# Batch 3's keys and queries loaded ahead of the down weights, and block sums at other places in VectorE's order

## The chip, the cores and the metric

The kernel runs on one core of one Trainium2 chip. The metric is the device time of one execution in microseconds, as the median of several runs. The profile is of one execution; its span is the time from the first to the last instruction, a little shorter than the device time.

Engine names as in the profile: PE is TensorE, PEld its weight loads, DVE VectorE, ACT ScalarE, POOL GpSimd, SP SyncE. DMAs that POOL issues are on queue q0, those of SP on q1; both are served by the same 16 DMA engines.

## What is computed

Sigmoid attention over 8 batches, 12 heads, 448 tokens, head size 64, and behind it a gated feed-forward layer (768 to 1536 to 768) over the 3584 tokens.

```
scores = scale * (q @ k^T) - log(S)
attn   = 1 / (1 + exp(-scores))
x      = (attn @ v), heads side by side            # [3584, 768]
gate   = max(x @ w_gate, 0);  val = x @ w_val
out    = (gate * val) @ w_out                       # float32
```

## The kernel before

All instructions of an engine run in the order in which the kernel's Python code emits them (a manual schedule), and the engines meet through semaphores. The order between attention and feed-forward work is written out by hand, batch by batch.

**Attention.** A batch's 12 heads go as three groups of four, its 448 tokens as seven chunks of 64, so a batch has 21 score units (group, chunk). `qk_unit` makes one unit: score matmuls into two PSUM banks (L239), a sigmoid on ACT (L187) into a tile PT. After a group's seven units `pv` (L257) multiplies with v and DVE copies the result, scaled, to `xT` (L184). PSUM has eight banks that are handed out in a ring, so each product waits until the bank that was given out eight allocations earlier has been read.

**Inputs.** `load` and `load_v` are DMAs on POOL's queue that convert to fp16. There is one buffer for keys and queries from batch 2 on (batch 1 has its own) and there are two for v; so a batch's keys can be loaded when the previous batch's have been rearranged. `dma_transposes(b, g)` rearranges keys and queries of group g on DVE (two copies into a tile `rel`, L222) and issues one DMA transpose on SP's queue (L226) into `qkT`. There are two `rel` buffers and three `qkT` buffers. `hold(b, g)` is a small copy on POOL that reads `qkT`, so that POOL's later DMA issues wait until that transpose has landed.

**Feed-forward.** For batch 0 and the first eight of 12 feature blocks of batch 0 and 1 the products are made in the plain or in a split form; later batches go in pairs. The split and paired forms are block products of Strassen's kind: seven products in place of eight, for which DVE makes sums of blocks ahead: `early_sum_steps` (weights, in batch 1), `split_sums` (batch 1's x, L391 X), `weight_sums(i)` (the down weights `wo`, L391 T), `token_sums` (four sums over hT, L441 and L391), `gate_sums` and `unit_sums`. `gv` is a plain unit: gate product, value product, ACT's relu (L334), DVE's product into `hT` (L343), which sets the value's bank free. `gv_split` is four units at once (L708 for PE, L719, L723 and L729 for DVE). `down_pair` is the output layer for two tiles of 128 tokens (PE L400; DVE L447 and L470; ACT L452), then stores on SP's queue.

**Order by batch.** A loop over `b` from 1 has stages `m`, each a burst of score units (`burst`) and then feed-forward work: in batch 1 `ffn_mix`, which pops plain units from a queue and emits, after each, one step of the early sums (from the second stage on); later `next_work`, which takes an item off `work` and emits `jobs` beside it. In batch 2 the items are the plain unit 8 (m = 0), the split units 0 to 3 (m = 1), plain unit 9 (m = 2), split 4 to 7 (m = 3), plain 10 and 11 (m = 4 and 5), all of batch 1's feed-forward. Batch 3 begins with `down_pair` of the first tiles. `prepare`, at the end of an item, emits the sums for the next one.

Before the change, DVE's order ran so: `split_sums(1)` after the plain unit of m = 0; the copies of `dma_transposes(3, 0)` and `(3, 1)` ahead of the unit of m = 4; `weight_sums(0)` and `(1)` after that unit; the token sums of the first tiles after the unit of m = 5; the copies of `(3, 2)` at the start of batch 3. POOL's order ran: v of batch 2, the down weights `wo`, then keys, queries and v of batch 3, then `hold(3, 2)` and batch 4's loads.

Of the kernel before, what the change touches and what calls it, by code (L numbers as in the profile page):

```python
# [18 lines left out]
def kernel(  # L19
# [10 lines left out]
    nc = tc.nc  # L30
# [82 lines left out]
    def load_v(b):  # L113
        v16 = tiles_of(b)[2]
        nc.gpsimd.dma_start(v16[:, 0::2, :], rows_of(v, b)[:, 0::2, :])
        for r in range(2):
            nc.gpsimd.dma_start(
                v16[64 - 64 * r : P - 64 * r, 1::2, :], rows_of(v, b)[64 * r : 64 * r + 64, 1::2, :]
            )
# [42 lines left out]
    def load_o():  # L162
        for m0, m1 in ((0, 512), (512, DM)):
            nc.gpsimd.dma_start(
                wo[:, :, m0:m1], moe_w_out[:, m0:m1].rearrange("(c p) m -> p c m", p=P)
            )
# [223 lines left out]
    def sub(o, a, b):  # L390
        nc.vector.tensor_tensor(out=o, in0=a, in1=b, op=AOP.subtract)  # L391
# [18 lines left out]
    def weight_sums(i):  # L410
        T = [late["T"][:, j] for j in range(4)]
        B11, B21 = wo[:, 0:HF, 0:HM], wo[:, HF:NFC, 0:HM]
        B12, B22 = wo[:, 0:HF, HM:DM], wo[:, HF:NFC, HM:DM]
        sub(T[i], *((B12, B11), (B22, T[0]), (B22, B12), (B21, T[1]))[i])
# [19 lines left out]
        return blocks  # L434

    def token_sums(g, p, k0=0, k1=HF):
        if ("y", g, p) not in sums:
            sums[("y", g, p)] = sums_tile(P)
        S1, S2, S4 = (t[:, k0:k1, :] for t in sums[("y", g, p)])
        A11, A12, A21, A22 = (t[:, k0:k1, :] for t in token_blocks(g, p))  # L440
        nc.vector.tensor_tensor(out=S1, in0=A21, in1=A22, op=AOP.add)  # L441
        sub(S2, S1, A11)
        sub(S4, A12, S2)
        sub(A21, A11, A21)

    def scaled(o, ps):
        nc.vector.tensor_scalar(  # L447
# [109 lines left out]
    def early_sum_steps(j, f):  # L557
        views = []
        for i in range(3 * j, 3 * j + 3):
            t = early.tile([P, 2, 512], FP16, tag=f"PT{i}", name="S")  # L560
            flat = t[:].rearrange("p a y -> p (a y)")[:, 0 : HD * 2 * P]
            views.append(flat.rearrange("p (x y) -> p x y", y=2 * P))
        yield lambda: gate_sums(f, f + 2)
        yield from unit_sum_steps(("s", f), f, views)
# [196 lines left out]
        c0, c1 = HALVES[half]  # L761
        push_gv(0, 64 * c0, 64 * (c1 - c0), fs, act_relu)

    def ffn_mix(count, hooks=(), steps=()):
        hooks = list(hooks)
        for left in range(count, -1, -1):
            while hooks and hooks[0][0] >= left:
                hooks.pop(0)[1]()
            if left:
                gv_queue.popleft()()  # L770
                for step in itertools.islice(steps, 1):
                    step()


# [80 lines left out]
    def hold(b, g):  # L855
        nc.gpsimd.tensor_copy(gate[0:1, :], qkT_tiles[(b, g)][0:1, 0, 0:2])
# [5 lines left out]
    def late_loads():  # L862
        dma_transposes(2, 2)
        hold(2, 2)
        load_v(2)
        load_o()


# [16 lines left out]
    def prepare():  # L885
        if work:
            kind, g, i = work[0]
            if kind == "w":
                unit_sums(("w", g, i), i)
            elif kind == "y":  # L890
                token_sums(g, i, 0, HF - 2 if FRESH.get(g) == i else HF)

    def next_work(jobs=(), alone=False, amid=None):
        kind, g, i = work.popleft()

        due = pending[:]
        del pending[:]

        def beside():
            for job in due + list(jobs):  # L900
                job()

        if kind == "y":
            down_pair(g, i, beside, prepare, not work, scaled_act if alone else scaled, amid)
        elif amid:
            raise ValueError(kind)
        elif kind == "w":
            gv_pair(g, i, lambda: (prepare(), beside()), nc.scalar.copy if alone else nc.vector.tensor_copy)
        elif kind == "s":
            gv_split(g, i, lambda: (prepare(), beside()))  # L910
        elif kind == "u":
            gv(g, 0, S, i, True)
            beside()
            prepare()
        else:
            beside()
            prepare()
            for m0, m1 in (DOWN_CUTS[i : i + 1] if g == 0 else ((0, 512), (512, DM))):
                down(g, 2 * NPP, m0, m1)

    for b in range(1, B):
        if b == 1:
            cuts, pv_at = (0, 3, 6, 9, 13, 17, 21), {3: (0, 2), 5: (1, 2)}
        else:
            cuts, pv_at = (0, 4, 7, 11, 14, 18, 21), {0: (-1, 2), 2: (0, 2), 4: (1, 2)}
        bursts = list(range(len(cuts) - 1))
        inner = {}
        if b > 2:
            inner = {0: 1, 3: 5} if b == 3 else {0: 1} if b % 2 == 0 else {2: 3, 3: 5} if b == B - 1 else {4: 5}
            for n in inner.values():  # L930
                bursts.remove(n)
        count = len(bursts)
        hooks = {}
        if b == 1:
            mix = (4, 3, 3, 3, 3, 4)
            hooks = {
                1: [(3, lambda: both(1, 1))],
                3: [(3, lambda: both(1, 2))],
                4: [(3, lambda: dma_transposes(2, 0)), (1, lambda: dma_transposes(2, 1))],
                5: [(4, late_loads)],  # L940
            }
            steps = itertools.chain.from_iterable(early_sum_steps(j, 2 * j) for j in range(4))
        else:
            mix = (0,) * count

        def burst(n):
            for i, (g, c) in enumerate(order[cuts[n] : cuts[n + 1]]):
                if n in pv_at and i == pv_at[n][1]:
                    if n == 0:
                        pv_finish(b - 1)  # L950
                        if b == 2:
                            push_group(0)
                        elif b % 2 == 0:
                            push_group(b // 2 - 1)
                    else:
                        pv_group(b, pv_at[n][0])
                qk_unit(b, g, c)

        if b == 3:
            dma_transposes(3, 2)  # L960
        for m in range(count):
            jobs = []
            burst(bursts[m])
            if m == 0 and b > 3:
                jobs.append(lambda: dma_transposes(b, 2))
            if b == 2 and m == count - 2:
                dma_transposes(3, 0)
                dma_transposes(3, 1)
            elif b == 3 and m == count - 1:
                jobs.append(lambda: dma_transposes(4, 1))  # L970
            elif 0 <= m - count + 2 and 3 < b < B - 1:
                jobs.append(lambda: dma_transposes(b + 1, m - count + 2))
            if b == 1:
                if m == 0:
                    load(2, 0, 1, "kq")
                    load(2, 1, 2, "kq")
                    load(2, 2, 3, "kq")
            elif m == 0 and b + 1 < B:
                if b == 3:
                    jobs.append(lambda: hold(3, 2))  # L980
                for g0, g1 in ((0, 1), (1, NG)) if b == 3 else ((0, NG),):
                    jobs.append(lambda g0=g0, g1=g1: load(b + 1, g0, g1, "kq"))
                jobs.append(lambda: load_v(b + 1))
            if b == 2 and m == 0:
                jobs.append(lambda: split_sums(1))
            elif b == 2 and m == 4:
                open_late()
                jobs.append(lambda: (weight_sums(0), weight_sums(1)))
            elif b == 3 and m == 0:
                jobs.append(lambda: (weight_sums(2), weight_sums(3)))  # L990
            elif b == 3 and m < 3:
                jobs.append(lambda: gate_sums(6 + 2 * m, 8 + 2 * m))
            if b % 2 and b > 2:
                if m == count - 1:
                    jobs.append(lambda: (batch_sums_t1(b // 2), batch_sums(b // 2, (0, 1))))
            elif b > 3 and m == 0:
                jobs.append(lambda: batch_sums(b // 2 - 1, (1, HD)))
            if mix[m]:
                for job in jobs:
                    job()  # L1000
                ffn_mix(mix[m], hooks.get(m, ()), steps if m else ())
            else:
                next_work(
                    jobs,
                    amid=(lambda: burst(inner[m])) if m in inner else None,
                )
            if b == 3 and m == count - 2:
                dma_transposes(4, 0)
# [35 lines left out]
```

## Time and profile before

| | |
|---|---|
| device time, median of 3 runs | 392.11 us (392.07 to 392.82) |
| profiled run: device time | 392.25 us |
| profiled run: span | 390.5 us |
| PE busy | 382.1 us |
| DVE busy | 299.6 us |
| ACT busy | 228.2 us |
| POOL busy | 50.0 us |
| granted TensorE clock, mean | 0.999 |

A row of the timeline reads: start and length in us, engine, line, operation, output<-inputs, shape, count, and in brackets the engine's idle time ahead of it with what ended it. Rows that follow one another closely are merged with a count. A length on PE holds pipelined matmuls, so the distance between two starts says more than the length. A row of DMA issues ends with the KB of one and the time from issue to landing; one that belongs to a line or tile gives the issue's own length in ns (least, median, most), then its start. A queue's row gives packets, MB and the share of 16 engines' time.

Batch 1's loop runs from about 30 to 61 us of the span, batch 2's from 61.7 to 97, batch 3's from 97 to 125.

### The profile page before, as it was taken

How to read it: one execution, taken by the hardware profiler on the slowest of the kernel's cores; microseconds unless marked ns; L12 is line 12 of the kernel's file. 1: busy time of each engine (PE TensorE's matmuls, PEld its weight loads, DVE VectorE, ACT ScalarE, POOL GpSimd, SP SyncE). 2: the span in 40 equal slices, each digit the busy share in tenths (PEclk: the TensorE clock that was granted, in tenths of full speed). 3: DMA queues.
4: the chain of work that ended last, by engine and by line, in shares of the span. 5: the costliest groups of instructions: out<-in, count | busy, mean ns of one | idle time of the engine just before them, and what ended most of it. 6: DMA issues, size and time to landing. Idle time of an engine off the chain costs nothing.

```text
span 390.5 us, 8971 instructions
## 1 busy us (share of the span) xinstructions
PE 382.1 (98%) x3576; PEld 223.8 (57%) x3576; DVE 299.6 (77%) x593; ACT 228.2 (58%) x482; POOL 50.0 (13%) x74
## 2 busy tenths in 40 slices
PE   7999999999999999999999999999999999999995
PEld 5678776884555545454555554545455555555663
DVE  3454666859867789999757789999987788999563
ACT  5967787567787755555547774545467354333321
POOL 9633305200220300003000300000000000000000
PEclk9999999999999999999999999999999999999999
DMA  9999997998499892225945694132002230000335
GB/s 179 198 200 204 204 184 128 205 203 141 71 210 229 159 219 34 48 49 70 187 91 129 122 227 76 29 65 43 10 21 74 72 81 1 2 0 2 81 86 159
DMA packets 68987, 43.81 MB, mean 112 GB/s; under 512 B 35664, under 2 KB 65616, under 8 KB 68944
## 3 DMA queue, kind: packets, MB, share of 16 engines
q0 software_dynamic: 30496, 23.24, 39.3%
q1 hardware_dynamic: 37664, 19.24, 23.3%
q10 hardware_dynamic: 784, 0.75, 0.6%
q8 instruction: 28, 0.46, 0.4%
q14 instruction: 15, 0.12, 0.1%
HBM read 47.19 MB, written 11.01 MB: 149 GB/s over the span
## 4 chain that ended last, share of the span: by engine, by line
PE 90%; ACT 4%; DVE 3%; DMA 1%; issue 1%; DVEq 0%; ACTq 0%
PE u L400 33%; PE g L400 16%; PE y L400 10%; PE qk_ps L239 8%; PE pv_ps L257 8%; PE g_ps L322 4%; PE v_ps L322 4%; ACT PT L187 3%; PE u L708 2%; PE g L708 1%; PE ya L366 1%; PE trt L204 1%; DMA ysb<-in_k_dram 1%; PE yb L366 1%; DVE S L391 1%
## 5 line engine op out<-in xcount | busy, mean ns | idle before, releaser
L187 ACT ACTIVATE PT<-qk_ps 128x448 f16<-128x448 f32 (+3 forms) x318 | 151.3, 585 | 81.3 <-PE qk_ps L239 80.8
L400 PEld LDWEIGHTS <-S 128*128 128x128 f16 x558 | 54.6, 98 | 45.3 <-issue 0.7
L627 DVE TENSOR_TENSOR gsb<-g,gsb 128x448 f32<-128x448 f32 x72 | 42.8, 624 | 10.1 <-PE g L400 9.6
L239 PE MATMUL qk_ps<-qkT 64*64 64x448 f16 (+2 forms) x756 | 47.8, 336 | 1.8 <-DMA qkT<-rel 0.7
L400 PEld LDWEIGHTS <-hT 128*128 128x128 f16 x306 | 28.5, 98 | 22.7 <-issue 5.2
L623 ACT COPY gsb<-u 128x448 f32<-128x448 f32 x48 | 25.6, 558 | 24.0 <-PE u L400 22.9
L257 PE MATMUL pv_ps<-PT,v 64*64 64x448 f16 (+2 forms) x756 | 37.3, 329 | 0.2 <-DVE hT L343 0.2
L184 DVE TENSOR_SCALAR xT<-pv_ps 128x448 f16<-128x448 f32 (+2 forms) x53 | 27.8, 566 | 9.6 <-PE pv_ps L257 8.4
L452 ACT ACTIVATE ysb<-u 128x384 f32<-128x384 f32 x30 | 14.7, 490 | 34.5 <-PE u L400 29.6
L400 PEld LDWEIGHTS <-wg 128*128 128x128 f16 x216 | 20.1, 98 | 21.8 <-issue 4.3
L400 PEld LDWEIGHTS <-wv 128*128 128x128 f16 x216 | 21.1, 98 | 19.7
L239 PEld LDWEIGHTS <-qkT 64*64 64x64 f16 x756 | 17.9, 105 | 22.4 <-issue 14.2
L470 DVE SCALAR_TENSOR_TENSOR ysb<-y,ysb 128x384 f32<-128x384 f32 x29 | 16.1, 556 | 17.9 <-PE y L400 10.4
L257 PEld LDWEIGHTS <-v 64*64 64x64 f16 x756 | 21.9, 107 | 11.2 <-issue 1.4
L400 PE MATMUL u<-T,hT 128*128 128x384 f16 x132 | 25.1, 327 | 0.0
L111 POOL DMA_DIRECT2D k<-in_k_dram x14 | 10.8, 774 | 108.1 <-DVE rel L222 103.0
L343 DVE TENSOR_TENSOR hT<-gate_sb,v_ps 128x256 f16<-128x256 f32 (+2 forms) x28 | 11.6, 419 | 16.6 <-ACT gate_sb L334 8.9
L400 PE MATMUL u<-xT,wg 128*128 128x448 f16 x108 | 23.5, 354 | 0.0
L400 PE MATMUL g<-xT,S 128*128 128x448 f16 x108 | 23.4, 352 | 0.0
L400 PE MATMUL u<-X,S 128*128 128x448 f16 x108 | 23.4, 352 | 0.0
L400 PE MATMUL g<-X,S 128*128 128x448 f16 x108 | 23.4, 352 | 0.0
L400 PE MATMUL u<-xT,wv 128*128 128x448 f16 x108 | 23.4, 352 | 0.0
(94 smaller groups left out, 574.6 us busy)
## 6 DMA issues: line engine op xcount, KB each, us to landing
out_dram<-ysb SPq DMA_DIRECT2D x52, 192.0 KB, 3.0
v<-in_v_dram POOLq DMA_DIRECT2D x8, 336.0 KB, 14.7
v<-in_v_dram POOLq DMA_DIRECT2D x16, 168.0 KB, 14.3
k<-in_k_dram POOLq DMA_DIRECT2D x4, 672.0 KB, 11.1
q<-in_q_dram POOLq DMA_DIRECT2D x4, 672.0 KB, 15.2
k<-in_k_dram POOLq DMA_DIRECT2D x9, 224.0 KB, 12.1
q<-in_q_dram POOLq DMA_DIRECT2D x7, 224.0 KB, 12.4
wo<-in_moe_w_out_dram POOLq DMA_DIRECT2D x1, 1536.0 KB, 12.1
```

What stands on the lines that cost most here:

```text
L184: nc.vector.tensor_scalar(out=xT, in0=src, scalar1=XSCALE, scalar2=None, op0=AOP.mult)
L187: nc.scalar.activation(PT_ap, ps_ap, AF.Sigmoid, bias=sig_bias, scale=qk_scale)
L239: nc.tensor.matmul(out_of(hh)[o : o + 64, :], qkT[rows, c, cols], qkT[rows, NCH + c0 : NCH + c1, cols], start=True, stop=True, tile_positi ...
L257: nc.tensor.matmul(ps[hh][64 * r : 64 * r + 64, 0:qn], v16[rows, 2 * g + hh, c * D : (c + 1) * D], pieces[c][rows, hh, :], start=(c == 0), ...
L322: nc.tensor.matmul(ps[:, 0:qn], (wg, wv)[i][:, dc, f * P : (f + 1) * P], xT_tiles[b][:, dc, q0 : q0 + qn], start=(dc == 0), stop=(dc == ND ...
L343: nc.vector.tensor_tensor(out=hT_tiles[g][:, f, o : o + qn], in0=gate_sb[:, 0:qn], in1=ps[1][:, 0:qn], op=AOP.mult,)
L400: nc.tensor.matmul(ps[:, 0:n], A[:, k_, :], W[:, k_, :], start=(first and k_ == 0), stop=(k_ == kn - 1), skip_group_check=True,)
L452: nc.scalar.activation(o, ps[:, 0:HM], AF.Copy, scale=OUT_SCALE)
L470: nc.vector.scalar_tensor_tensor(out=o, in0=ps[:, 0:HM], scalar=OUT_SCALE, in1=o, op0=AOP.mult, op1=AOP.add)
L623: by(gs[u][i][:], ps[u][:, 0:S])
L627: nc.vector.tensor_tensor(out=gs[u][i][:], in0=ps[u][:, 0:S], in1=gs[u][i][:], op=AOP.add)
L708: nc.tensor.matmul(ps[j // 2][:, j % 2 * SQ : (j % 2 + 1) * SQ], sets[j][i][:, k_, :], W[:, k_, :], start=(first and j % 2 == 0 and k_ == ...
```

## The change

Six edits, all of order; the arithmetic is the same.

- In batch 1 `ffn_mix` takes a list `given`: how many early-sum steps follow each unit. The sixteen steps start in the first stage in place of the second.
- Batch 3's keys and queries are loaded after batch 2's v and ahead of `wo`; they came after `wo`.
- A list `ahead` of jobs is emitted before an item's own work, where `jobs` are emitted in it or after it. `split_sums(1)` goes ahead at m = 0 of batch 2; `weight_sums(0)` ahead at m = 4 and `weight_sums(1)` ahead at m = 5.
- `dma_transposes(3, 0)` goes ahead at m = 2, `(3, 1)` beside the item of m = 3, `(3, 2)` ahead at m = 5.
- The four token sums of the first tiles are split: the first goes ahead at m = 5 (after `weight_sums(1)`, before the copies of `(3, 2)`), the other three after that item.
- `hold(3, 2)` ahead of batch 4's loads is gone.

```diff
-    def ffn_mix(count, hooks=(), steps=()):
+    def ffn_mix(count, hooks=(), steps=(), given=()):
...
-                for step in itertools.islice(steps, 1):
+                for step in itertools.islice(steps, given[count - left] if steps else 0):
                     step()
...
         load_v(2)
+        load(3, 0, NG, "kq")
         load_o()
...
-                token_sums(g, i, 0, HF - 2 if FRESH.get(g) == i else HF)
+                if (g, i) != (0, 0):
+                    token_sums(g, i, 0, HF - 2 if FRESH.get(g) == i else HF)
...
+        for job in ahead:
+            job()
         if kind == "y":
...
+            given = ((0, 1, 1, 0), (1, 1, 0), (1, 1, 1), (1, 1, 0), (2, 1, 0), (1, 1, 1, 1))
...
-        if b == 3:
-            dma_transposes(3, 2)
         for m in range(count):
-            jobs = []
+            jobs, ahead = [], []
...
-            if b == 2 and m == count - 2:
-                dma_transposes(3, 0)
-                dma_transposes(3, 1)
+            if b == 2 and m == 2:
+                ahead.append(lambda: dma_transposes(3, 0))
+            elif b == 2 and m == 3:
+                jobs.append(lambda: dma_transposes(3, 1))
...
-                if b == 3:
-                    jobs.append(lambda: hold(3, 2))
-                for g0, g1 in ((0, 1), (1, NG)) if b == 3 else ((0, NG),):
+                for g0, g1 in ((0, 1), (1, NG)) if b == 3 else ((0, NG),) if b > 3 else ():
                     jobs.append(lambda g0=g0, g1=g1: load(b + 1, g0, g1, "kq"))
...
             if b == 2 and m == 0:
-                jobs.append(lambda: split_sums(1))
+                ahead.append(lambda: split_sums(1))
             elif b == 2 and m == 4:
                 open_late()
-                jobs.append(lambda: (weight_sums(0), weight_sums(1)))
+                ahead.append(lambda: weight_sums(0))
+                first_sums = token_sum_steps(0, 0)
+            elif b == 2 and m == 5:
+                ahead += [lambda: weight_sums(1), first_sums[0], lambda: dma_transposes(3, 2)]
+                jobs += first_sums[1:]
...
-                ffn_mix(mix[m], hooks.get(m, ()), steps if m else ())
+                ffn_mix(mix[m], hooks.get(m, ()), steps, given[m])
             else:
                 next_work(
-                    jobs,
+                    jobs, ahead=ahead,
```

`token_sum_steps` returns the four sums of `token_sums` as separate steps.

More of the change, by code (lines that the diff above doesn't have):

```diff
@@ L436, in token_sums, with token_sum_steps @@
     def token_sums(g, p, k0=0, k1=HF):
+        for step in token_sum_steps(g, p, k0, k1):
+            step()
+    def token_sum_steps(g, p, k0=0, k1=HF):
         if ("y", g, p) not in sums:
@@ L440, in token_sums @@
         A11, A12, A21, A22 = (t[:, k0:k1, :] for t in token_blocks(g, p))
[L441 to L444, printed above, removed]
+        return (
+            lambda: nc.vector.tensor_tensor(out=S1, in0=A21, in1=A22, op=AOP.add),
+            lambda: sub(S2, S1, A11),
+            lambda: sub(S4, A12, S2),
+            lambda: sub(A21, A11, A21),
+        )
     def scaled(o, ps):
@@ L890, in prepare, with next_work @@
             elif kind == "y":
-                token_sums(g, i, 0, HF - 2 if FRESH.get(g) == i else HF)
-    def next_work(jobs=(), alone=False, amid=None):
+                if (g, i) != (0, 0):
+                    token_sums(g, i, 0, HF - 2 if FRESH.get(g) == i else HF)
+    def next_work(jobs=(), alone=False, amid=None, ahead=()):
         kind, g, i = work.popleft()
```

## The prediction

> **What bounds the kernel now.** I read the page's first part, then the waits of the tensor engine (PE), and then the timeline at the place of each wait.
>
> ```profile
> PE 382.1 (98%) x3576; PEld 223.8 (57%) x3576; DVE 299.6 (77%) x593; ACT 228.2 (58%) x482; POOL 50.0 (13%) x74
> ...
> PE qk_ps L239 <- DMA qkT<-rel: 0.7, 1, 0.7
> PE qk_ps L239 <- ACT ysb L452: 0.6, 1, 0.6
> PE u L400 <- DVE ysb L447: 0.4, 1, 0.4
> PE pv_ps L257 <- DVE hT L343: 0.2, 1, 0.2
> ```
>
> PE is busy 382.1 of 390.5 us, so whatever an edit on VectorE (DVE), POOL or the DMA queues is worth must come out of PE's few gaps. Between the first and the fourth batch there are four such waits, about 1.9 us together. The change moves no matmul; it can only close these gaps, or open new ones. I go through the gaps in order of time. PE's row has the idle time in brackets; since ends of matmuls are modelled, each may be 0.1 off.
>
> **Batch 1, sums moved forward.** `given` replaces one step after every feed-forward unit. In the fifth stage it is (2, 1, 0): two steps after the first unit, where one stood.
>
> ```profile
> 55.17 1.51 PE L257 MATMUL pv_ps<-PT,v 64*64 64x448 f16 x26 [0.20 <-DVE hT L343]
> 53.96 0.42 DVE L343 TENSOR_TENSOR hT<-gate_sb,v_ps 128x256 f16<-128x256 f32 x1 [2.66 <-ACT gate_sb L334]
> 54.77 0.35 DVE L343 TENSOR_TENSOR hT<-gate_sb,v_ps 128x192 f16<-128x192 f32 x1
> 55.03 0.55 DVE L578 TENSOR_TENSOR S<-S,wg 128x768 f16<-128x768 f16 x1
> ```
>
> DVE stood idle 2.66 us for ScalarE's gate at 53.96, so coming earlier with other sums buys nothing there. The product `pv` waits for a PSUM bank that the second hT (54.77, ends 55.12) sets free, and goes on at 55.17. With two sums ahead of that hT instead of one, it comes one L578 later: +0.55. The third hT, behind it, frees the bank of the next scores, and shifts by the same. The other stages keep a product between any two sums, or stand where DVE idles, and I cost them at nothing; the first stage now has two sums between hT products that are followed by score tiles needing their banks, cover that I read as some tenths. Bounds of this part: 0 (if PE's later work had slack that I don't see) to 0.6. I take +0.55.
>
> **Batch 2, split sums ahead of the first unit.**
>
> ```profile
> 68.15 1.31 PE L708 MATMUL g<-X,S 128*128 128x224 f16 x12
> 69.60 1.31 PE L708 MATMUL u<-X,S 128*128 128x224 f16 x12
> 70.75 1.31 PE L708 MATMUL g<-xT,wg 128*128 128x224 f16 x12
> ...
> 66.47 0.62 DVE L343 TENSOR_TENSOR hT<-gate_sb,v_ps 128x448 f16<-128x448 f32 x1 [1.67 <-PE v_ps L322]
> 67.01 0.50 DVE L391 TENSOR_TENSOR X<-xT 128x672 f16<-128x672 f16 x1
> ...
> 68.93 1.15 DVE L719 COPY gsb<-u 128x448 f32<-128x448 f32 x2
> ```
>
> Twelve such matmuls take 1.15 (69.60 to 70.75), but 68.15 to 69.60 is 1.45: a hidden gap of 0.30. The product at 69.60 adds onto `u`, which L719 must first copy out; L719 starts at 68.93 because the four X sums stand before it from 67.01. Moved ahead, they use the 1.67 us in which DVE waited for v_ps: DVE was free from 64.80, the sums take 1.92 (67.01 to 68.93), so they end at 66.7, the hT slips 0.25 and L719 starts as soon as `u` is there. Gain 0.30.
>
> **Batch 3's first transposes, and the order before batch 3.**
>
> ```profile
> 97.25 0.57 PE L239 MATMUL qk_ps<-qkT 64*64 64x448 f16 x8 [0.66 <-DMA qkT<-rel]
> 102.01 1.14 PE L400 MATMUL u<-T,S 128*128 128x384 f16 x6 [0.43 <-DVE ysb L447]
> ...
> L226 SPq DMA_TRANSPOSE qkT<-rel x1: 1511/1511/1511, 92.6 to 92.6; - x1
> DMA to landing us min/median/max: 4.6/4.6/4.6
> ...
> 91.88 0.38 DVE L222 COPY rel<-k 128x896 f16<-128x896 f16 x1
> 93.63 0.62 DVE L343 TENSOR_TENSOR hT<-gate_sb,v_ps 128x448 f16<-128x448 f32 x1 [0.46 <-PE v_ps L322]
> 94.17 1.35 DVE L391 TENSOR_TENSOR T<-wo 128x2304 f16<-128x2304 f16 x1
> 97.08 0.62 DVE L343 TENSOR_TENSOR hT<-gate_sb,v_ps 128x448 f16<-128x448 f32 x1 [0.16 <-ACT gate_sb L334]
> 99.27 0.55 DVE L391 TENSOR_TENSOR hT<-hT 128x768 f16<-128x768 f16 x1
> 100.34 1.15 DVE L184 TENSOR_SCALAR xT<-pv_ps 128x448 f16<-128x448 f32 x2
> 101.41 0.55 DVE L447 TENSOR_SCALAR ysb<-u 128x384 f32<-128x384 f32 x1
> ```
>
> The transpose (3,0) is issued at 92.6 and lands 4.6 later, at 97.2, when PE's scores of batch 3 start. Moved two stages forward it is issued near 80. The 0.66 goes.
>
> At 102.01 PE waits for L447, which stands behind four token sums (to 99.82), the copies of (3,2) and two xT. The change takes the first token sum and the (3,2) copies out from between the last hT (97.08, set by ScalarE's gate and thus not moved) and xT. The last sum ends 0.6 sooner, at 99.2; xT follows it at once instead of at 100.34, 1.1 sooner, and L447 ends near 101.96 - 1.1 = 100.85. PE, 0.66 earlier, wants it at 102.01 - 0.43 - 0.66 = 100.92. Gain 0.43; at worst 0.15 of it stays.
>
> What is moved must fit further up. Ahead of the hT of 93.63 the four rel copies (1.3, from 91.88) give place to one T sum (1.35): even. Between 94.17 and 97.08 stood two T sums (2.8 with the hT's end); there now stand one T sum, one token sum and two rel copies, 1.35 + 0.55 + 0.7 = 2.6. Even too.
>
> **Batch 4's loads, without the hold.**
>
> ```profile
> 125.34 0.57 PE L239 MATMUL qk_ps<-qkT 64*64 64x448 f16 x8 [0.56 <-ACT ysb L452]
> ...
> L226 SPq DMA_TRANSPOSE qkT<-rel x1: 4110/4110/4110, 116.8 to 116.8; - x1
> DMA to landing us min/median/max: 8.5/8.5/8.5
> ...
> 104.64 0.17 POOL L856 COPY gate<-qkT 1x2 f16<-1x2 f16 x1 [33.64 <-DMA qkT<-rel]
> ```
>
> The wait at 125.34 is put down to ScalarE, but the transpose (4,0), issued at 116.8 and landing 8.5 later at 125.3, fits to 0.1: I read it as the cause. Alone a transpose took 4.6; this one shared the queues with batch 4's loads. POOL held these loads until 104.64 for (3,2). Without `hold(3,2)`, and with the (3,2) copies done near 97, POOL issues them some 7.5 us sooner, so they are through before 116. The transpose then lands near 121, four us early. Gain 0.56. (3,2) itself now runs beside those loads; its reader is the burst just ahead of 116.8, so it has some 17 us.
>
> **The queue: what the load order costs.** Keys and queries of batch 3 go ahead of the down weights `wo`, and two transposes run while `wo` is loading. This is the unknown price.
>
> ```profile
> 65.32 2.07 POOL L164 DMA_DIRECT2D wo<-in_moe_w_out_dram  x2
> 68.18 0.85 POOL L111 DMA_DIRECT2D q<-in_q_dram  x1
> ...
> wo<-in_moe_w_out_dram POOLq DMA_DIRECT2D x1, 768.0 KB, 15.6
> ...
> q<-in_q_dram POOLq DMA_DIRECT2D x1, 672.0 KB, 20.5
> ...
> 77.38 1.16 DVE L184 TENSOR_SCALAR xT<-pv_ps 128x448 f16<-128x448 f32 x2
> ...
> q0 software_dynamic: 171, 0.14, 87.2%
> q1 hardware_dynamic: 204, 0.05, 34.2%
> ...
> L226 SPq DMA_TRANSPOSE qkT<-rel x1: 1640/1640/1640, 130.0 to 130.0; - x1
> DMA to landing us min/median/max: 12.3/12.3/12.3
> ...
> q1 hardware_dynamic: 3381, 0.86, 79.6%
> ```
>
> `wo`'s second half (issued about 66.4) lands at 82.0, q of batch 3 at 68.2 + 20.5 = 88.7; so k and q, 1344 KB, take 6.7, and `wo`, 2304 KB, some 11.5 at that rate. In the new order q lands at 88.7 - 11.5 = 77.2 at the latest, ahead of the copies, which stand behind the xT that ends at 78.5. `wo` lands at 82.0 + 6.7 = 88.7, plus 0.55 because the whole queue starts behind batch 1, plus what the transposes take. In the microsecond from 121 to 122, when loads (q0) and a transpose (q1) ran together, the queues moved 171 and 204 packets: about one for one, though a load's packet is large and costs more time. So a transpose creeps beside loads: the one at 130, issued into batch 5's loads, took 12.3 to land. Two transposes alone fill 79.6% of the 6 us from 92 to 98, 4.8. By about 92, then, (3,0) is through and little of (3,1): half of 4.8, 2.4. `wo` lands at 91.65. DVE comes to its T sum at 91.9 + 0.25 = 92.1, and has 0.46 to spare before the hT. Cost nothing, with a margin of 0.8; bounds 0 and, with all 4.8 in front (94.05 against 92.5), 1.55. I take 0, as the 12.3 row is the same situation.
>
> [...]
>
> **Sum.** +0.55 - 0.30 - 0.66 - 0.43 - 0.56 = -1.40 on a span of 390.5. The profiled run took 392.25, 1.75 more than its span, against a median of 392.11. So 392.11 - 1.40 = 390.7.
>
> **The rivals.**
> 1. The added sum in batch 1 costs nothing. For it: DVE's rows there are close, and PE's wait is only 0.20 now. Against: the bank is freed by that very hT. Then 390.15.
> 2. `wo` lands late because both transposes are served in front: DVE's T sum starts 1.55 late, and behind it in DVE's order stand two hT, the token sums, xT and L447, for which PE waits. 392.11 - 1.40 + 1.55 = 392.25. For it: the margin is under a microsecond; against: the 12.3 us of the transpose beside loads.
> 3. Slower: the copies of (3,2) need the buffer that (3,0) is read from, of which there are two. They now stand ahead of the last hT. If (3,0), issued near 80, lands after 96, DVE stops there with the hT, three token sums, xT and L447 behind it, and PE's scores wait as well. By 12.3 it lands at 92. Were it to creep half as long again, behind `wo`'s larger packets (18.5, to 98.3), the price is 2.3: 393.0. It decides from a landing at 96, and the time passes the old one from 97.5.
> 4. The change doesn't do what it says: behind each removed wait stands the next constraint at the same time (for 125.34, ScalarE's copy at L452, as the row says; for 97.25, the gate). Then about 392.1. Against it: the same transitions at other batches show no wait.
>
> **Numbers.** Forecast 0.52 (own range 390.3 to 391.2), rival 1 0.12, rival 2 0.16, rival 3 0.10, rival 4 0.10. A change under 0.2%, 0.8 us, can't be told from none. Faster: forecast and rival 1, 0.64. Same: rival 4 and three quarters of rival 2, 0.22. Slower: rival 3 and the rest of 2, 0.14. The range goes from rival 1 with a little to spare, 390.0, to just over rival 2, 392.5; outside is rival 3 and some of 1 and 2.
>
> **What would show it.** PE's waits lose "DMA qkT<-rel" and the ScalarE entry, and L447's shrinks; the pitch at the first split unit falls from 1.45 to 1.15; `pv` at 55 shows an idle time of about 0.7 in place of 0.20. `wo`'s second half lands before 92.5, and the first T sum has no idle ahead of it. The transpose (4,0) lands in under 5 us. The forecast is wrong if that T sum, or the (3,2) copies, show an idle time put down to a DMA.

## The result, and the profile after

The changed kernel takes 391.07 us (median of 9 runs, 390.6 to 391.27), the kernel before 392.39 (9 runs, 391.88 to 393.41). The ratio is 0.9964 with a 95% interval of 0.9953 to 0.9974: faster by 1.0 to 1.8 us. The forecast was 390.7 against 392.11, or 1.4 less; taken off the later median of 392.39, the same 1.4 gives 391.0. The profiled span fell from 390.5 to 388.9.

The longest of PE's waits after the change (who waited for whom: us in total, times, longest):

```profile
PE warm_ps L175 <- DVE zeros L130: 1.2, 1, 1.2
PE pv_ps L257 <- DVE hT L343: 0.8, 1, 0.8
PE qk_ps L239 <- ACT PT L187: 0.3, 1, 0.3
```

The entries for the DMA, for ScalarE's L452 and for L447 (now L453) are gone; the one for `pv` has grown from 0.2 to 0.8. Line numbers behind the first edit are 6 higher than before. The rows of PE's timeline that answer to those shown of before:

```profile
55.62 1.51 PE L257 MATMUL pv_ps<-PT,v 64*64 64x448 f16 x26 [0.79 <-DVE hT L343]
...
68.60 1.31 PE L714 MATMUL g<-X,S 128*128 128x224 f16 x12
69.75 1.31 PE L714 MATMUL u<-X,S 128*128 128x224 f16 x12
...
96.67 0.57 PE L239 MATMUL qk_ps<-qkT 64*64 64x448 f16 x8
...
99.87 1.14 PE L400 MATMUL y<-T,S 128*128 128x384 f16 x6
101.05 1.14 PE L400 MATMUL u<-T,S 128*128 128x384 f16 x6
...
117.01 1.14 PE L400 MATMUL y<-T,S 128*128 128x384 f16 x6
117.98 1.14 PE L400 MATMUL u<-T,S 128*128 128x384 f16 x6
...
123.75 0.57 PE L239 MATMUL qk_ps<-qkT 64*64 64x448 f16 x8
```

The split unit's products now follow at 1.15. The y product of the next pair takes 0.97 (117.01 to 117.98), so between 99.87 and 101.05 some 0.2 of a wait is left that is too short for the list. VectorE's rows show where part of it comes from:

```profile
93.17 1.36 DVE L391 TENSOR_TENSOR T<-wo 128x2304 f16<-128x2304 f16 x1 [1.06 <-issue]
94.45 0.61 DVE L343 TENSOR_TENSOR hT<-gate_sb,v_ps 128x448 f16<-128x448 f32 x1
...
97.32 0.61 DVE L343 TENSOR_TENSOR hT<-gate_sb,v_ps 128x448 f16<-128x448 f32 x1
...
100.45 0.54 DVE L453 TENSOR_SCALAR ysb<-u 128x384 f32<-128x384 f32 x1
```

The first T sum stands idle 1.06 us. The list calls that "issue", but the DMA rows name it: the second part of `wo` is issued at about 68.1 and lands 25.0 later, at 93.1.

```profile
wo<-in_moe_w_out_dram POOLq DMA_DIRECT2D x1, 768.0 KB, 25.0
```

**How starts are compared.** Each execution starts a little differently: the first loads land earlier or later (the two 128 KB loads of q took a median of 5.0 us to land in the kernel before, 5.6 in the changed one), and PE's position at 50 us differs by -0.3 to +0.5 from that of the kernel before in the runs below, including kernels that are alike up to there. From 28 us on that offset is constant until the first step. So each step below is the start of a PE row minus the start of the same row in the kernel before, less that difference at the row of 50.65 us. Negative is earlier.

```
PE row of before      after   e1    e2    e3    e4    e5    e6    e7    e8    e9
offset at 50.65       -0.14 +0.51 +0.04 +0.17 -0.27 +0.54 +0.07 -0.22 -0.05 +0.19
pv            55.17   +0.60  0.00 -0.47 +0.59 +0.60 +0.59  0.00 +0.59 -0.47  0.00
u<-X          69.60   +0.29 -0.30 -0.79 +0.59 +0.29 +0.29  0.00 +0.28 -0.80  0.00
v_ps          95.29   +0.29 -0.21 -0.28 +0.59 +0.29 +0.29  0.00 +0.29 -0.79  0.00
qk, batch 3   97.25   -0.44 -0.94 -1.01 -0.15 -0.43 +0.29 -0.02 -0.44 -1.52 -0.03
u<-T         102.01   -0.82 -0.99 -1.06 -0.62 -0.90 -0.15  0.00 -0.92 -1.99 -0.01
qk, batch 4  125.34   -1.45 -1.62 -1.69 -1.24 -1.53 -0.78 +0.74 -1.54 -2.62 -0.63
```

The row of 55.17 begins with the third matmul of its `pv`; in e2 and e8, where `pv` runs in one piece, that matmul is compared. Values may be 0.01 off. The steps of the changed kernel are the differences down its column: +0.60, -0.31, -0.73, -0.38, -0.63, together -1.45. Nothing changes after batch 4's start.

### The profile page after: what moved, and what is told of

It reads as the page before. It is cut to its first block, busy times and chain, and to the rows that moved or that the text cites. A ratio compares the mean times of both kernels' runs of the same rounds, so it can differ in the third digit from the quotient of the medians.

```text
span 388.9 us, 8970 instructions
## 1 busy us (share of the span) xinstructions
PE 382.0 (98%) x3576; PEld 223.6 (58%) x3576; DVE 299.4 (77%) x593; ACT 227.9 (59%) x482; POOL 50.0 (13%) x73
## 4 chain that ended last, share of the span: by engine, by line
PE 93%; ACT 3%; DVE 1%; DMA 1%; issue 1%; DVEq 0%; ACTq 0%
PE u L400 34%; PE g L400 16%; PE y L400 11%; PE qk_ps L239 9%; PE pv_ps L257 8%; PE g_ps L322 5%; PE v_ps L322 4%; ACT PT L187 3%; PE u L714 2%; PE g L714 2%; PE ya L366 1%; PE trt L204 1%; PE yb L366 1%; DMA ysb<-in_k_dram 1%; DVE S L391 0%
## 5 line engine op out<-in xcount | busy, mean ns | idle before, releaser
L400 PE MATMUL u<-T,hT 128*128 128x384 f16 x132 | 25.1, 327 | 0.0
L400 PE MATMUL g<-xT,wg 128*128 128x448 f16 x108 | 23.4, 352 | 0.0
L400 PE MATMUL u<-X,wv 128*128 128x448 f16 x108 | 23.4, 352 | 0.0
## 6 DMA issues: line engine op xcount, KB each, us to landing
wo<-in_moe_w_out_dram POOLq DMA_DIRECT2D x1, 1536.0 KB, 18.2
```

The source lines that it names most:

```text
L400: nc.tensor.matmul(ps[:, 0:n], A[:, k_, :], W[:, k_, :], start=(first and k_ == 0), stop=(k_ == kn - 1), skip_group_check=True,)
```

## The experiments

Nine kernels. Times with an interval are of five rounds against the kernel before, whose median beside them was 392.42 to 392.62; the others are one execution, read by their trace.

**e1: one sum in place of two in batch 1.**

```diff
-            given = (..., (1, 1, 0), (2, 1, 0), (1, 1, 1, 1))
+            given = (..., (1, 1, 0), (1, 1, 1), (1, 1, 1, 1))
```

> The changed kernel, but with one sum after the first unit of batch 1's fifth stage in place of two (given (1, 1, 1) there; one sum more goes behind the stage's last unit). Theory: the second sum is what makes pv wait 0.79 us in the changed kernel in place of 0.20 before; pv's wait goes back to about 0.20, every later PE start moves 0.55 to 0.6 us earlier, the span falls from 388.9 to about 388.3 and the ratio to the kernel before from 0.996 to about 0.995. Rival: ScalarE's gates set this place, and the time stays within 0.1 us of the changed kernel's span.

391.20 us, ratio 0.9964 (0.9952 to 0.9977): the same as the changed kernel. The wait did go back, but the gain did not reach the end. PE's rows of e1:

```profile
55.68 1.51 PE L257 MATMUL pv_ps<-PT,v 64*64 64x448 f16 x26 [0.20 <-DVE hT L343]
...
101.53 0.65 PE L400 MATMUL u<-T,S 128*128 128x384 f16 x3 [0.38 <-DVE ysb L453]
```

`pv` is where it was before the change, 0.60 earlier than with the change, and PE keeps 0.5 to 0.6 of that as far as batch 3. At 101 it waits 0.38 for L453, and in the table only 0.17 is left. So the theory was right about the place and wrong about the end, where 0.55 to 0.6 was expected: a PE that comes sooner meets the T sum that waits for `wo`, whose landing did not move (25.1 us after its issue, 25.0 in the changed kernel).

**e2: no sum between the hT products of that stage.**

```diff
-            given = (..., (1, 1, 0), (2, 1, 0), (1, 1, 1, 1))
+            given = (..., (1, 1, 1), (0, 0, 2), (1, 1, 1, 1))
```

> The changed kernel, but no sum stands between the hT products of batch 1's fifth stage: one is emitted behind the fourth stage's last unit, where VectorE is idle, and two behind the fifth stage's last unit (given (1, 1, 1), (0, 0, 2) for these stages). Theory: pv's wait of 0.79 us falls to 0.1 or less, later PE starts come 0.8 to 1.1 us earlier than in the changed kernel, span about 387.9 to 388.1, ratio about 0.993 to 0.994. Rival: the two sums now delay xT, whose bank the next stage's second unit needs, and 0.3 us or more comes back as a new PE wait there.

390.54 us, ratio 0.9944 (0.9930 to 0.9958), span 388.8 where 387.9 to 388.1 was expected. PE's rows of e2:

```profile
54.48 1.77 PE L257 MATMUL pv_ps<-PT,v 64*64 64x448 f16 x28
...
95.05 1.29 PE L322 MATMUL v_ps<-xT,wv 128*128 128x448 f16 x6 [0.35 <-DVE hT L343]
...
100.99 1.14 PE L400 MATMUL u<-T,S 128*128 128x384 f16 x6 [0.38 <-DVE ysb L453]
```

`pv` now runs in one piece, 1.07 us earlier than in the changed kernel. The new wait in the next stage that the rival foresaw does not come; but 0.8 is paid back at 95 (the hT behind the late T sum) and at 101 (L453 behind it). By the table 0.24 is left at the end. The intervals of e2 and the changed kernel overlap, and the trace shows no more than the table does.

**e4: the hold put back.**

```diff
             elif m == 0 and b + 1 < B:
+                if b == 3:
+                    jobs.append(lambda: hold(3, 2))
```

> The changed kernel with hold(3, 2) put back ahead of batch 4's loads. Theory of the prediction: the hold is what made the loads collide with the transpose (4, 0); with it the loads start only when (3, 2) has landed, (4, 0) lands in about 8 us again and PE waits about 0.6 us at the start of batch 4; span 389.5. Rival: (3, 2) is now issued at 97.6 and, alone on the queues, lands in 4 to 5 us, near 102, so the loads start some 3 us earlier than in the kernel before and end before the collision costs anything; the wait is under 0.15 us and the span within 0.2 of 388.9. Then it is the earlier copies of (3, 2), not the lost hold, that closed the gap.

390.44 us, span 388.7, offset -0.27. POOL's row for the first of batch 4's loads, then the transpose (4, 0) (length in ns, start) with its time to landing, and PE's start of batch 4:

```profile
102.65 0.75 POOL L111 DMA_DIRECT2D k<-in_k_dram  x1 [0.57 <-DVE T L391]
...
L226 SPq DMA_TRANSPOSE qkT<-rel x1: 3352/3352/3352, 115.6 to 115.6; - x1
DMA to landing us min/median/max: 6.9/6.9/6.9
...
123.54 0.57 PE L239 MATMUL qk_ps<-qkT 64*64 64x448 f16 x8
```

With the hold the loads start at 102.65 in place of 97.40, the transpose takes 6.9 in place of 5.0, and still lands a microsecond ahead of its reader. No wait. The rival holds: given the earlier copies of (3, 2), taking the hold out was worth nothing.

**e9: the kernel before, with the hold alone taken out.**

```diff
-                if b == 3:
-                    jobs.append(lambda: hold(3, 2))
```

> The kernel before without hold(3, 2). The hold kept in the changed kernel cost nothing, since the copies of (3, 2) come at 96.7 there. Theory: what closes the gap at batch 4 is the time at which batch 4's loads start, and either edit alone does it: without the hold they start at about 100.5 in place of 105.2, (4, 0) lands in about 5 us and the wait of 0.56 goes, span about 389.9; the other waits stay. Rival: 3 to 4 us are not enough with (3, 2) beside the loads; the wait stays above 0.3.

391.82 us, span 390.0.

```profile
100.60 0.75 POOL L111 DMA_DIRECT2D k<-in_k_dram  x1 [29.41 <-DVE rel L222]
...
L226 SPq DMA_TRANSPOSE qkT<-rel x1: 2877/2877/2877, 116.9 to 116.9; - x1
DMA to landing us min/median/max: 5.0/5.0/5.0
...
124.90 0.57 PE L239 MATMUL qk_ps<-qkT 64*64 64x448 f16 x8
```

The loads start at 100.60, the transpose lands in 5.0, and batch 4 starts 0.63 earlier, just the step that the changed kernel shows. Either edit alone closes this gap: what counts is how long ahead of the transpose (4, 0) batch 4's loads start, by whatever means. That was 11.6 us in the kernel before, 12.9 in e4 (102.65 to 115.59), 16.3 here and 18.4 in the changed kernel, and from 12.9 on PE does not wait.

**e5: the transposes at their old place, the loads at their new one.**

```diff
-            if b == 2 and m == 2:
-                ahead.append(lambda: dma_transposes(3, 0))
-            elif b == 2 and m == 3:
-                jobs.append(lambda: dma_transposes(3, 1))
+            if b == 2 and m == 4:
+                dma_transposes(3, 0)
+                dma_transposes(3, 1)
```

> The changed kernel with (3, 0) and (3, 1) issued where they were before, ahead of the unit of batch 2's m = 4; the loads keep their new order. Theory: the second half of wo, free of transposes, lands at 88.7 to 89.0 in place of 93.1 (68.1 + 25.0), so these transposes cost the loads 4.2 us and not 2.4; the first T sum starts without an idle for a DMA, but PE waits again at the start of batch 3, for the transpose or the sums behind four rel copies, 0.7 to 1.6 us in all; span 389.6 to 390.5. Rival: wo's lateness comes from its own place in the queue; it lands at 92 or later without transposes too.

392.10 us, span 390.2, offset +0.54. The DMA row of `wo`'s second part in e5, and PE's wait:

```profile
wo<-in_moe_w_out_dram POOLq DMA_DIRECT2D x1, 768.0 KB, 20.8
...
PE qk_ps L239 <- DMA qkT<-rel: 0.7, 1, 0.7
```

From the same place in the queue `wo` takes 20.8 in place of 25.0: the two transposes beside it cost the loads 4.2 us. (It takes 21.0 in e6, also without transposes, and 25.1, 24.8 and 24.4 in e1, e2 and e4, so about 4.) It lands at 89.6, where 88.7 to 89.0 was expected; its issue came 0.7 later in this execution. The wait at batch 3's start is back, and with it 0.7 of the gain. That wait is thus removed by the earlier transposes, not by the loads.

**e6: the kernel before, with the loads alone moved.** As in the change's diff, `load(3, 0, NG, "kq")` stands before `load_o()` and no longer at its old place; nothing else is changed.

> The kernel before with one part of the change: batch 3's keys and queries loaded ahead of wo; the transposes stay where they were. Theory: nothing waits for these loads at the old place of the copies (91.9), and wo, with no transpose beside it, lands at 88.7 to 89, ahead of the first T sum at 94.2: all three waits stay (0.66, 0.43, 0.56) and the span is within 0.15 of 390.5 once the start-up offset is taken off. Rival: the shorter queue behind makes something earlier; span 0.3 or more below.

393.08 us, span 391.3. Up to 102 the rows are those of before to 0.02 us, as expected, but at batch 4 PE lost 0.74, so the span is 0.7 above the 390.5 of the kernel before, start-up offset taken off, where it was expected within 0.15:

```profile
105.62 0.75 POOL L111 DMA_DIRECT2D k<-in_k_dram  x1 [0.73 <-DVE ysb L470]
...
126.16 0.57 PE L239 MATMUL qk_ps<-qkT 64*64 64x448 f16 x8 [1.30 <-DMA qkT<-rel]
```

POOL's first load for batch 4 was issued 0.45 later than before, the transpose took 9.2 instead of 8.5, and the wait of 0.56 grew to 1.30. Why POOL was later was not tried; it is one execution. The three numbers suggest how steeply this wait hangs on the loads' lead over the transpose (4, 0): a lead of 11.3 us costs 1.3, 11.6 costs 0.56, 12.9 and more nothing.

**e7: `wo` in whole rows.**

```diff
-        for m0, m1 in ((0, 512), (512, DM)):
-            nc.gpsimd.dma_start(
-                wo[:, :, m0:m1], moe_w_out[:, m0:m1].rearrange("(c p) m -> p c m", p=P)
-            )
+        nc.gpsimd.dma_start(wo[:], moe_w_out.rearrange("(c p) m -> p c m", p=P))
```

> The changed kernel with wo loaded by one DMA of whole rows in place of two column parts; a packet then carries 1536 bytes in place of 1024 or 512. In the changed kernel loads and transposes move packet for packet from 83 us on, just while the 512-byte part is loading, and wo lands at 93.1. Theory: with half as many packets wo loses fewer turns, lands by 91.5 or earlier, the first T sum has no idle for a DMA, and the wait left at 101 (0.2) goes: span 0.1 to 0.3 below 388.9. Rival: the turns go by bytes or by time, and wo lands at 92.5 or later as before.

390.81 us, ratio 0.9956 (0.9942 to 0.9970), span 388.7. What the two queues moved from 84 to 89 us, when transposes and `wo` ran together (packets, MB, share of 16 engines' time), in the changed kernel:

```profile
q0 software_dynamic: 1187, 0.61, 87.8%
q1 hardware_dynamic: 1188, 0.30, 46.0%
```

and the same in e7, with its `wo` and its first T sum (lines 3 lower than in the changed kernel):

```profile
q0 software_dynamic: 623, 0.83, 92.8%
q1 hardware_dynamic: 623, 0.16, 23.9%
...
wo<-in_moe_w_out_dram POOLq DMA_DIRECT2D x1, 2304.0 KB, 23.4
...
91.94 1.35 DVE L388 TENSOR_TENSOR T<-wo 128x2304 f16<-128x2304 f16 x1
93.70 0.62 DVE L340 TENSOR_TENSOR hT<-gate_sb,v_ps 128x448 f16<-128x448 f32 x1 [0.41 <-PE v_ps L319]
...
97.14 0.62 DVE L340 TENSOR_TENSOR hT<-gate_sb,v_ps 128x448 f16<-128x448 f32 x1 [0.48 <-ACT gate_sb L331]
...
99.78 1.14 PE L397 MATMUL y<-T,S 128*128 128x384 f16 x6
100.87 1.14 PE L397 MATMUL u<-T,S 128*128 128x384 f16 x6
```

In these five microseconds the two queues move packet for packet: 1187 against 1188, and 623 against 623. In the changed kernel there is one transpose packet of 256 bytes (0.30 MB in 1188) to each 512-byte packet of `wo`'s second part (0.61 MB in 1187). In e7, where a row of `wo` has 1536 bytes, the loads' packets hold 1332 on the mean (0.83 MB in 623), so 0.39 as many transpose packets go beside the same data, and the loads move 0.83 MB in place of 0.61. The bytes are not shared equally: 0.61 against 0.30 MB, and 0.83 against 0.16. Small packets alone are not the reason: in e5, with no transpose beside them, the loads moved at 197 GB/s from 84 to 88, where 0.61 MB in 5 us are 122, and `wo`'s second part took 3.0 us more than its first from issue to landing (20.8 against 17.8), in the changed kernel 6.8 more (25.0 against 18.2). `wo`, issued at 67.0, lands at 90.4, and the T sum starts without idle. The transposes pay for it and land later (15.8 us in place of 13.4 for the first), which nothing waits for.

At PE little of this can be seen. The step at 102 is -0.48 in place of -0.38, and of the 0.2 that was left there 0.1 stays (99.78 to 100.87, less 0.97). e4, whose `wo` is loaded as in the changed kernel, has a step of -0.47 as well: in that execution `wo` landed at 92.3 in place of 93.1, and its T sum idled only 0.40.

```profile
92.38 1.36 DVE L391 TENSOR_TENSOR T<-wo 128x2304 f16<-128x2304 f16 x1 [0.40 <-issue]
```

The intervals of e7 and the changed kernel overlap too. What the larger packets are worth to PE is shown only by e8.

**e8: e2 and e7 together.**

> e2_steps_behind with wo loaded by one DMA of whole rows. In e2 PE came 0.95 us earlier to the first T sum than in the changed kernel, but got back 0.9 of it as waits for hT and L453, behind wo's landing. Theory: with wo landing by 91.5 most of it stays; ratio to the kernel before about 0.992 to 0.993 (e2: 0.9944), PE's start of batch 4 about 2.2 to 2.5 us earlier than before once the start-up offset is taken off. Rival: something else holds PE at the same place and the ratio stays at 0.9944.

389.83 us, ratio 0.9931 (0.9919 to 0.9944), span 387.8. PE's waits in e8:

```profile
PE warm_ps L172 <- DVE zeros L130: 1.2, 1, 1.2
PE qk_ps L236 <- ACT PT L184: 0.3, 1, 0.3
PE qk_ps L236 <- DVE qkT L208: 0.2, 1, 0.2
```

The list has no wait between 50 us and the fourth batch any more; about 0.1 is left at the product of 102, too short for it. Batch 4 starts 2.62 us sooner than before, 1.17 sooner than in the changed kernel. That settles e2, and with it e1: the sums' order was worth 1.07 at `pv`, and it was `wo`'s landing that held it back. Of the two kernels that have `wo` in whole rows, e8 is 1.08 ahead of e7 at batch 4; of the two that have it in parts, e2 is 0.24 ahead of the changed kernel. The expectation had e2 0.95 ahead at the T sum; by the table it is 1.08, of which 0.84 is paid back. e8 beats both kernels; its interval lies below that of the changed kernel.

**e3: the split sums behind the plain unit again.**

```diff
-                ahead.append(lambda: split_sums(1))
+                jobs.append(lambda: split_sums(1))
```

> The changed kernel with split_sums(1) back behind the plain unit of batch 2's first stage. Theory: the copy L725 of the first split unit comes behind the four X sums again, the starts of its third and second product lie 1.45 us apart in place of 1.15, and every later PE start moves 0.3 us; but at the first T sum, where VectorE idles 1.06 us for wo, that much is taken up again, so that the start of batch 4 comes only 0 to 0.15 us later than in the changed kernel, start-up offset taken off. Rival: all 0.3 us is still there at the end.

391.31 us, span 389.5. PE's rows show the pitch of 1.45 again, and further on the pitch at 101:

```profile
68.91 1.31 PE L714 MATMUL g<-X,S 128*128 128x224 f16 x12
70.36 1.31 PE L714 MATMUL u<-X,S 128*128 128x224 f16 x12
...
100.47 1.14 PE L400 MATMUL y<-T,S 128*128 128x384 f16 x6
101.56 1.14 PE L400 MATMUL u<-T,S 128*128 128x384 f16 x6
```

By the table PE is 0.30 later than with the change from 69.60 on, and batch 4 still starts 0.21 later. That lies between the theory (0 to 0.15) and the rival (0.3), so neither holds as it stands. I had expected VectorE's idle of 1.06 for `wo` to swallow the 0.3; but in the changed kernel only 0.2 is waited at 101 (101.05 - 99.87 - 0.97), here 0.1 still is (101.56 - 100.47 - 0.97), and so only 0.1 is taken up again.

## Why the prediction was right, step by step

**Batch 1.** Forecast +0.55, measured +0.60. e1 takes out the one sum and the wait is back at 0.20. The stages before cost nothing, as assumed: PE's difference to the kernel before is the start-up offset up to there.

**Split sums.** -0.30 forecast, -0.31 measured; e3 brings back the pitch of 1.45 and 0.30 at this place, of which 0.21 reaches batch 4.

**Batch 3's transposes.** -0.66 forecast, -0.73 measured. The row's idle time was 0.1 short, as the prediction warned for modelled ends. e5 shows that the transposes did it, and e6 that the loads alone do not. The loads had to come first all the same: in the kernel before, q of batch 3 landed at 88.7, and the transpose (3, 0) now starts at 79.3.

**L447.** -0.43 forecast, -0.38 measured, for the reasons given. The row of before that stands ahead of 102.01 shows that the list's 0.43 was not all of the wait:

```profile
100.44 1.14 PE L400 MATMUL y<-T,S 128*128 128x384 f16 x6
```

From 100.44 to 102.01 are 1.57, 0.60 more than the 0.97 without a wait; 0.2 of that is left after the change. L453 ended at 100.99 and not at 100.85, since the last hT came at 97.32 behind the late T sum. About half of what is left has another cause, since it stays in e7.

**Batch 4.** -0.56 forecast, -0.63 measured. The collision of loads and (4, 0) was read rightly, against the list of waits, which named ScalarE. The credit to the lost hold was not right: e4 shows that the hold could have stayed, and e9 that its loss alone would have been enough. The prediction named both edits in one sentence and counted 0.56 once, so the sum is not touched.

**The queue.** This is the term that was mis-sized. The prediction took 2.4 us for what the transposes cost `wo`, and a landing at 91.65 with a margin of 0.8; they cost 4.2 (e5), `wo` landed at 93.1 and the T sum idled 1.06. The prediction had named an idle time of that sum for a DMA as a sign that the forecast is wrong. The sign came, and this step did fail, though the total held.

The prediction read from its row of 121 to 122 that a load's packet costs much more time than a transpose's: 87.2% for 171 against 34.2% for 204, three times as much. `wo`'s second part has packets of 512 bytes, and there it is only 1.9 times (87.8% for 1187 against 46.0% for 1188, in the changed kernel from 84 to 89), which fits a higher price of each transpose packet beside it. In addition both queues all but stopped for about 0.8 us (17 GB/s, last section); how much of the 4.2 that makes was not tried.

Of the idle of 1.06 only some 0.1 reached PE. e7 shows where the rest went: without the idle, the two hT behind the T sum wait 0.41 for PE's v_ps and 0.48 for ScalarE's gate, so VectorE has 0.9 to spare there. The prediction had counted the first (its 0.46) and not the second, so it is in part luck that the second rival (+1.55) stayed far off. e1 and e2 show the same term from behind: most of what brings PE there sooner is paid back.

**Rival 3** was never near. The transpose (3, 0) of the changed kernel:

```profile
L226 SPq DMA_TRANSPOSE qkT<-rel x1: 3899/3899/3899, 79.3 to 79.3; - x1
DMA to landing us min/median/max: 13.4/13.4/13.4
```

It landed at 92.7, four us ahead of the copies that need its buffer (96.72). **Rivals 1 and 4** fell with e1 and with the steps.

## What to carry to other kernels

When several waits of the bound engine are removed at once, ask which event of fixed time (here a load's landing) stands behind them: beyond it most of each further gain is paid back (e1, e2), and an edit of which 0.24 us reaches the end may keep its whole microsecond once that event is moved (e8 against e7). Where a large load must run beside many small packets, give the load larger packets, since here the two queues moved packet for packet, with load packets of 512 bytes (1187 to 1188) as with those of 1332 (623 to 623). And take the start-up offset off before comparing single executions: here it was as large as the effects.

## What was not expected of the hardware

Both DMA queues nearly stopped together for about 0.8 us while a transpose and loads ran side by side. From the changed kernel, busy time in stretches (engines, then granted clock, DMA share, GB/s; the share adds up both queues and can exceed 1):

```profile
84.00:89.00 5.00, 5.00 (x54) 4.84 (x51) 3.87 (x7) 1.11 (x3) 0.00 (x0) 1.00 1.35 186
90.00:90.75 0.75, 0.75 (x20) 0.47 (x16) 0.75 (x2) 0.75 (x3) 0.00 (x0) 1.00 0.47 17
91.50:95.00 3.50, 3.50 (x28) 1.58 (x27) 2.44 (x5) 2.95 (x8) 0.00 (x0) 1.00 1.25 194
```

186 and 194 GB/s stand on either side of 17; from 90.00 to 90.75 the loads' queue moved 16 packets and the transposes' 18. The kernel before, whose transposes run later, moved 192 GB/s in the same stretch. The cause is open.

The issue of the transpose (3, 0) on SP took 3.9 us in the changed kernel, against 1.5 alone in the kernel before, so beside the loads the issue was slower as well as the transfer (13.4 us to landing against 4.6).
